# Moving weight loads and small steps between the units of a fused adaLN attention and gated MLP kernel

## The chip, the cores and the metric

The kernel runs on one core of a Trainium2 chip. The metric is the device time of one execution in microseconds. Before the change it was 1273.58 us, the median of three runs (1273.51 to 1275.47).

Engine names in profiles: PE multiplies matrices (PEld loads its weights), DVE is the vector engine, ACT the scalar engine, POOL is GpSimd. SP only issues DMAs here. Each engine works through its own list of instructions in order.

## The reference

The shapes are: 2048 rows of width D = 448; H = 16 heads of width 256 with 2048 cached keys and values each; a hidden width of 1792 in the MLP. Everything is bf16.

```
mod = (silu(c) @ w_mod) in six parts: sa, ca, ga, sb, cb, gb
h = layernorm(x) * (1 + ca) + sa
q = h @ wq, by heads;  p = softmax(q @ K^T / 16);  o = p @ V
x = x + ga * (o @ wo)
h = layernorm(x) * (1 + cb) + sb
x = x + gb * ((gelu(h @ w_gate) * (h @ w_up)) @ w_down)
```

## The kernel before

**Units.** The rows fall into four chunks of 512 (`r`). A unit `u` is one head `h` on one chunk: 64 units, the four chunks of a head next to each other. A unit has 16 steps `j`, one for each 128 keys. In a step the PE computes transposed scores `st` for two steps ahead (L321, two matmuls), ACT makes `E = exp(st)` (L462), the DVE adds E to `esum` (L503), and the PE multiplies V by E into two PSUM tiles `oT` (L506, two matmuls). At the end of a unit the DVE and ACT copy one oT tile each to `oTn` (L468, L469), and `esum` makes a trip through DRAM to be transposed: `scr<-esum` (L473), `esT<-scr` (L478).

**Behind the unit.** In the next unit the row sums are taken at step 7 (`inv`, L482), and the output projection follows in four tiles (`wo_tile`: matmuls L330, an add into x_acc on the DVE, L335) at steps 8, 10, 12 and 14. So the projection of a unit lies one unit behind its attention.

**Order.** The program's order on each engine is written out by hand. `fill(u, j, f)` puts a piece of work `f` behind the matmuls of step j of unit u; pieces of one slot run in the order in which they were filed. In the same way `mf(r, k, f)` puts a piece behind tile k of chunk r in the MLP. A step's pieces run before its `wo_tile`. At step 15 the query projection for the same chunk of the next head runs (`q_proj`, L307, eight matmuls); the last head has no next one, so its four units have none.

**PSUM tiles** come from pools: three of the tag `st`, two of `oT`, three of `mi`. The tiles of q_proj, wo_tile and of the modulation all use `mi`.

**Norms.** A norm of a chunk is split in pieces: `stats` (four, DVE), `rstd` (POOL), `norm` (four, DVE), `twin` (DVE), then either `transpose` on the PE or `turn`, and `modulate` (four, DVE, L268). `turn` is a trip through DRAM on SP's queue: `xscr<-xn` (L259) and four transposing loads `hT<-xscr` (L262), each of which waits for that store. Chunk 0 and 1 of the first norm use the PE; chunk 2 is turned at step 1 of unit 1 and wanted at step 12 and 13 of it, chunk 3 likewise in unit 2. The second norm's chunk 0 and 1 are done in units 62 and 63, chunk 2 and 3 in the MLP.

**Loads.** All but two early loads go through SP's queue. `load_wm` loads columns of w_mod; the first 960 are loaded at once, and the rest right behind the first head's K. `ld` (L410) loads K of head h+1 by two transposing DMAs at step 0 of the first unit of head h; `ld2` (L413) loads V and wo of head h+1 and wq of head h+2 one unit later. wq's load includes a small memset on POOL. `mod_rep` (L205) makes ga or gb from w_mod, `scale_wo` (L137) multiplies wo by ga on POOL, `mod_cols` (L184) makes sb and cb.

**MLP.** For each chunk, 14 tiles of 128 hidden columns are made in pairs by `gate_up`: gate and up matmuls (L543 with 64 rows, L550), gelu on ACT (L555), the product on the DVE (`hhT`, L556). The gate tile uses the tag `st`; the up tile uses `oT`, but every third, counted by `nu`, uses `mi`. Then `down` multiplies by w_down (L563) in four tiles. The first pair of the next chunk (`lead`) is put ahead of `down`. The last unit's output projection lies within the first chunk of the MLP.

Of the kernel before, what the change touches and what calls it, by code (L numbers as in the profile page):

```python
# [17 lines left out]
def kernel(  # L18
# [15 lines left out]
    nc = tc.nc  # L34
    S = A_x.shape[1]
    D = A_x.shape[2]
# [9 lines left out]
    NHC = Df // P  # L46
# [22 lines left out]
        fill=0.0, base=0, channel_multiplier=1,  # L69
# [6 lines left out]
    WA = 2 * D + 64  # L76
# [4 lines left out]
    x_acc = [res.tile([P, 4, D], F32, name=f"x_acc{r}") for r in range(NC)]  # L81
# [22 lines left out]
    def load_wq(h):  # L104
        wq_t = wts.tile([P, DCH, Dh], BF16, name="wq_t")
        nc.gpsimd.memset(wq_t[DL:P, 3, :], 0.0)
        nc.sync.dma_start(
            out=wq_t[:, 0:3, :],
            in_=A_wq[0:384, h * Dh:(h + 1) * Dh].rearrange("(c p) d -> p c d", p=P),
        )  # L110
        nc.sync.dma_start(out=wq_t[:DL, 3, :], in_=A_wq[384:D, h * Dh:(h + 1) * Dh])
        return wq_t
# [24 lines left out]
    def scale_wo(wo_t):  # L137
        for cc in range(2):
            nc.gpsimd.tensor_tensor(out=wo_t[:, cc, :], in0=wo_t[:, cc, :], in1=ga_bf[:], op=ALU.mult)  # L139

    def load_x(eng, r):
        eng.dma_start(
            out=x_bf[r], in_=x2d[r * 512:(r + 1) * 512, :].rearrange("(t p) d -> p t d", p=P)
        )

    def load_wm(a, b):
        nc.sync.dma_start(out=wm[:, 0:3, a:b], in_=w_mod[0:384, a:b].rearrange("(c p) n -> p c n", p=P))
        nc.sync.dma_start(out=wm[:DL, 3, a:b], in_=w_mod[384:D, a:b])
# [7 lines left out]
    wq[0] = load_wq(0)  # L156
    kTs[0] = load_k(0, parts=2)
    wos[0] = load_wo(0)
    load_wm(WA, 6 * D)
    load_x(nc.sync, 2)  # L160
    load_x(nc.sync, 3)
    wq[1] = load_wq(1)


    cps = mi_tile([P, DCH], F32, "cps")
# [18 lines left out]
    def mod_cols(g0):  # L184
        mps_ = mi_tile([P, 2 * DCH], F32, "modc")
        for v in range(2):
            for m in range(DCH):
                o = (g0 + v) * D + m * P
                for k in range(DCH):
                    nc.tensor.matmul(  # L190
                        mps_[:, v * DCH + m:v * DCH + m + 1],
                        lhsT=wm[:, k, o:o + P], rhs=scT[:, k:k + 1],
                        start=(k == 0), stop=(k == DCH - 1),
                    )
        return mps_

    def mod_cols_out(mps_, s_c, c1p_c):
        nc.vector.tensor_copy(out=s_c[:], in_=mps_[:, 0:DCH])
        nc.vector.tensor_single_scalar(out=c1p_c[:], in_=mps_[:, DCH:2 * DCH], scalar=1.0, op=ALU.add)
        nc.vector.tensor_copy(out=s_c[DL:P, 3:4], in_=mps_[0:DL, 3:4])  # L200
        nc.vector.tensor_single_scalar(
            out=c1p_c[DL:P, 3:4], in_=mps_[0:DL, 2 * DCH - 1:2 * DCH], scalar=1.0, op=ALU.add
        )

    def mod_rep(g, tgt):  # L205
        mp = mi_tile([P, D], F32, "mp")
        for k in range(DCH):
            nc.tensor.matmul(
                mp[:], lhsT=scT_rep[:, k, :], rhs=wm[:, k, g * D:(g + 1) * D],
                start=(k == 0), stop=(k == DCH - 1),  # L210
            )
        nc.vector.tensor_copy(out=tgt[:], in_=mp[:])
# [114 lines left out]
    def wo_tile(h, r, t, oTn, inv):  # L327
        wps = mi_tile([P, D], F32, "wps")
        for dc in range(2):
            nc.tensor.matmul(  # L330
                wps[:], lhsT=oTn[:, dc, t * P:(t + 1) * P], rhs=wos[h][:, dc, :],
                start=(dc == 0), stop=(dc == 1),
            )
        prev = x_bf[r] if h == 0 else x_acc[r]
        nc.vector.scalar_tensor_tensor(  # L335
            out=x_acc[r][:, t, :], in0=wps[:], scalar=inv[:, t:t + 1],
            in1=prev[:, t, :], op0=ALU.mult, op1=ALU.add,
        )
# [19 lines left out]
    fills = {}  # L358

    def fill(u, j, f):  # L360
        fills.setdefault((u, j), []).append(f)
# [4 lines left out]
            nc.vector.tensor_copy(out=scT_rep[:, k, :], in_=scT[:, k:k + 1].to_broadcast((P, P)))  # L366

    fill(0, 11, rep)
    fill(0, 13, lambda: mod_rep(2, ga_bf))
    fill(0, 14, lambda: scale_wo(wos[0]))  # L370
    fill(3, 10, lambda: mod_rep(5, gb_bf))
    fill(4, 9, lambda: mod_cols_out(mod_cols(3), sb_c, cb1p_c))

    def add_ln(key, src, c1p, s, js, jn, jt, jm=None):
        box = {}

        def stats(t):
            if t == 0:
                box["l"] = LN(key, src, c1p, s, mi_tile)
            box["l"].stats(t)  # L380

        for t in range(4):
            fill(*js[t], lambda t=t: stats(t))
        fill(*js[3], lambda: box["l"].rstd(0, 4))
        for t in range(4):
            fill(*jn[t], lambda t=t: box["l"].norm(t))
        fill(*jn[3], lambda: box["l"].twin(nc.vector))
        if jm is None:
            for p_ in range(2):
                fill(*jt[p_], lambda p_=p_: box["l"].transpose(p_))  # L390
        else:
            fill(*jt, lambda: box["l"].turn())
            for ch in range(DCH):
                fill(*jm[ch], lambda ch=ch: box["l"].modulate(ch))

    def at(u, *js):
        return [(u, j) for j in js]
# [9 lines left out]
    for u, (h, r) in enumerate(units):  # L407
        if h + 1 < H:
            if r == 0:
                def ld(h=h):  # L410
                    kTs[h + 1] = load_k(h + 1)

                def ld2(h=h):  # L413
                    vs[h + 1] = load_v(h + 1)
                    wos[h + 1] = load_wo(h + 1)
                    if h + 2 < H:
                        wq[h + 2] = load_wq(h + 2)
                fill(u, 0, ld)
                fill(u + 1, 0, ld2)
            if r == 3:  # L420
                fill(u, 0, lambda h=h: scale_wo(wos[h + 1]))
            fill(u, 15, lambda h=h, r=r: q_proj(h + 1, r))
        if h == H - 1 and r in (2, 3):
            jm = at(u + 1, 4, 6, 8, 10) if r == 2 else [("mlp", ch) for ch in range(DCH)]
            add_ln(("b", r - 2), x_acc[r - 2], cb1p_c, sb_c, at(u, 0, 2, 4, 6), at(u, 8, 9, 10, 11),
                   (u, 11), jm)


    mlpw = {}
# [61 lines left out]
    pend = None  # L491
    for u, (h, r) in enumerate(units):
        oT = [aps.tile([P, 512], F32, tag="oT", bufs=2, name=f"oT{i}") for i in range(2)]
        esum = espool.tile([P, 512], BF16, name="esum")
        for j in range(NKS):
            g = u * NKS + j
            emit_st(g + 2)
            emit_exp(g + 1)
            E = Es[g]
            if j == 1:  # L500
                nc.vector.tensor_tensor(out=esum[:], in0=Es[g - 1][:], in1=E[:], op=ALU.add)  # L501
            elif j > 1:
                nc.vector.tensor_tensor(out=esum[:], in0=esum[:], in1=E[:], op=ALU.add)  # L503
            Es.pop(g - 1, None)
            for i in range(2):
                nc.tensor.matmul(  # L506
                    oT[i][:], lhsT=vs[h][:, j, i * P:(i + 1) * P], rhs=E[:],
                    start=(j == 0), stop=(j == NKS - 1),
                )
            if j == NKS - 1:  # L510
                oTn, sums = finish_unit(u, oT, esum)
            for f in fills.pop((u, j), ()):
                f()
            if pend is not None:
                ph, pr, po, psums = pend[:4]
                if j == 7:
                    pinv = psums()
                if j in (8, 10, 12, 14):
                    wo_tile(ph, pr, (j - 8) // 2, po, pinv)
                if j == 14:  # L520
                    pend = None
        pend = (h, r, oTn, sums)


    wgu, wd = mlpw["gu"], mlpw["d"]

    nu = [0]

    def gate_up(r, fc0, hhT):
        hr = hT[("b", r)]  # L530
# [46 lines left out]
    def mf(r, k, f):  # L577
        mfill.setdefault((r, k), []).append(f)

    ph, pr, po, psums = pend  # L580
    box = {}
    mf(0, 5, lambda: box.update(inv=psums()))
    for t in range(4):
        mf(0, 5 + 1 + t, lambda t=t: wo_tile(ph, pr, t, po, box["inv"]))
        mf(0, NHC - 4 + t, fills.pop(("mlp", t))[0])
    for r in range(2, NC):
        for t in range(4):
            mf(r - 2, NHC + t, lambda r=r, t=t: ln2(r).stats(t))
            mf(r - 1, 3 + t, lambda r=r, t=t: ln2(r).norm(t))
            mf(r - 1, NHC - 2 + t // 2, lambda r=r, t=t: ln2(r).modulate(t))  # L590
        mf(r - 1, 2, lambda r=r: ln2(r).rstd(0, 4))
        mf(r - 1, 6, lambda r=r: (ln2(r).twin(nc.vector), ln2(r).turn()))
    lns = {}

    def ln2(r):
        if r not in lns:
            lns[r] = LN(("b", r), x_acc[r], cb1p_c, sb_c, mi_tile)
        return lns[r]
# [48 lines left out]
```

The softmax here doesn't subtract the row's maximum and nothing guards it: scores larger than these inputs give would overflow.

## Time and profile before

| what | value |
|---|---|
| median of three runs | 1273.58 us |
| the profiled execution's own time | 1273.87 us |
| its span, first to last instruction | 1272.1 us |
| mean granted PE clock | 0.996 |
| idle PE in the stretch 0 to 36 us | 9.3 us |
| 36 to 62 us (clock 0.90) | 7.3 us |
| 62 to 84.7 us (clock 0.97) | 0.5 us |
| 84.7 to 1078.5 us | 0.8 us |
| 1078.5 to 1124.7 us | 0.7 us |
| 1124.7 to 1133.2 us (clock 0.80) | 3.2 us |
| 1133.2 to 1228.2 us | 4.2 us |
| 1228.2 to 1272.1 us | 3.3 us |

The idle times are the length of each stretch less the busy time of the PE in it. The stretches are: unit 0 and what leads to it; unit 1; unit 2; units 3 to 60; 61 to 63; the first pair of the MLP; its first three chunks; the last chunk.

How to read what follows. In a list of waits a line names who waited, for what, and then the total in us, the number of times and the longest. In a timeline a line gives the start, the length, the engine (SPq is SP's queue), the line of the kernel, the operation, what it writes and reads, and how often; in brackets the idle time before it and what ended it. Matmuls overlap, so the time between two starts says more than the length of one: 0.216 us is the usual distance for 512 columns, and 0.427 us at half clock. Buffer numbers such as oT_511 tell apart the tiles of one name.

### The profile page before, as it was taken

To read this page: it belongs to the slowest core of one execution; us is meant where nothing else is said; L and a number is where in the kernel's file an instruction comes from. 1 tells how busy PE (TensorE), PEld (TensorE's weight loads), DVE (VectorE), ACT (ScalarE), POOL (GpSimd) and SP (SyncE) were. 2 spreads that over 40 slices of the span, in tenths; PEclk is the share of its full clock that TensorE was granted. 3 is DMA by queue.
4 is the path that set the end of the run, shared out by engine and by line. 5 is a ranking of instruction groups with operands and counts; after the bars stand their busy time and mean duration, and the time that the engine had idled before them with its cause. 6 is when DMAs were issued, how large, how long until landed. Compare 5 with 4: busy or idle time off the path is not lost.

```text
span 1272.1 us, 17345 instructions
## 1 busy us (share of the span) xinstructions
PE 1242.7 (98%) x5900; PEld 562.5 (44%) x5900; DVE 797.2 (63%) x1697; ACT 705.4 (55%) x1217; POOL 69.6 (5%) x87
## 2 busy tenths in 40 slices
PE   7799999999999999999999999999999999989998
PEld 3344444444444444444444444444444444434443
DVE  6666666656666666666666666666666666765543
ACT  4455656665655666666566666556666666642222
POOL 1100000000102001010000000000000000000000
PEclk9899999999999999999999999999999999999999
DMA  9312122372204040312222221304040310120110
GB/s 255 90 50 64 51 47 61 50 212 45 73 16 91 17 98 17 85 30 51 61 46 65 51 64 29 87 13 94 17 98 18 72 36 13 38 59 15 48 44 19
DMA packets 180170, 75.98 MB, mean 60 GB/s; under 512 B 149873, under 2 KB 170546, under 8 KB 180082
## 3 DMA queue, kind: packets, MB, share of 16 engines
q1 hardware_dynamic: 179024, 73.38, 24.5%
q10 hardware_dynamic: 1058, 1.51, 0.5%
q8 instruction: 46, 0.75, 0.2%
q14 instruction: 42, 0.34, 0.1%
HBM read 33.18 MB, written 13.37 MB: 37 GB/s over the span
## 4 chain that ended last, share of the span: by engine, by line
PE 92%; DVE 3%; DMA 3%; issue 1%; SPq 1%; ACT 1%; POOL 0%; DVEq 0%
PE st L321 33%; PE qps L307 8%; PE wps L330 7%; PE dps L563 3%; PE g_ps L550 3%; PE u_ps L550 3%; DMA scr<-esum 1%; PE g_ps L543 1%; DVE esum L503 1%; DMA wm<-in_w_mod_dram 0%; DMA xscr<-xn 0%; DMA esT<-scr 0%; DVE hT L268 0%; DVE bst L225 0%; SPq L262 0%
## 5 line engine op out<-in xcount | busy, mean ns | idle before, releaser
L462 ACT ACTIVATE E<-st 128x512 bf16<-128x512 f32 x1024 | 598.2, 599 | 287.4 <-PE st L321 277.4
L321 PE MATMUL st<-qT,kT 128*128 128x512 bf16 x2048 | 609.6, 379 | 1.1 <-ACT qT L314 1.1
L503 DVE TENSOR_TENSOR esum<-esum,E 128x512 bf16<-128x512 bf16 x896 | 394.5, 440 | 126.1 <-ACT E L462 93.3
L506 PEld LDWEIGHTS <-v_h 128*128 128x128 bf16 x2048 | 200.2, 98 | 247.5 <-issue 13.8
L321 PEld LDWEIGHTS <-kT 128*128 128x128 bf16 x2048 | 200.1, 98 | 232.0 <-issue 5.4
L330 PE MATMUL wps<-wo_t,oTn 128*128 128x448 bf16 x512 | 138.9, 353 | 0.0
L307 PE MATMUL qps<-hT,wq_t 128*128 128x512 bf16 x512 | 125.0, 385 | 5.7 <-DVE hT L268 5.2
L555 ACT ACTIVATE gl<-g_ps 128x512 bf16<-128x512 f32 x56 | 33.4, 597 | 98.1 <-PE g_ps L550 98.1
L314 ACT CAST qT<-qps 128x512 bf16<-128x512 f32 x64 | 37.5, 585 | 86.2 <-PE qps L307 86.2
L139 POOL TENSOR_TENSOR wo_t<-wo_t,ga_bf 128x448 bf16<-128x448 bf16 x32 | 34.9, 1110 | 889.3 <-DMA wo_t<-in_A_wo_dram 823.3
L307 PEld LDWEIGHTS <-wq_t 128*128 128x128 bf16 x512 | 50.5, 99 | 68.8 <-issue 10.5
L330 PEld LDWEIGHTS <-oTn 128*128 128x128 bf16 x512 | 50.2, 98 | 60.7 <-issue 0.6
L501 DVE TENSOR_TENSOR esum<-E 128x512 bf16<-128x512 bf16 x64 | 27.1, 423 | 75.5 <-ACT E L462 75.5
L556 DVE TENSOR_TENSOR hhT<-gl,u_ps 128x512 bf16<-128x512 bf16 x56 | 38.5, 687 | 48.2 <-PE u_ps L550 48.2
L335 DVE SCALAR_TENSOR_TENSOR x_acc_93<-wps,inv,x_acc_93 128x448 f32<-128x448 f32 x60 | 41.0, 684 | 40.7 <-PE wps L330 40.7
L335 DVE SCALAR_TENSOR_TENSOR x_acc_94<-wps,inv,x_acc_94 128x448 f32<-128x448 f32 x60 | 41.0, 684 | 40.3 <-PE wps L330 40.3
L335 DVE SCALAR_TENSOR_TENSOR x_acc_92<-wps,inv,x_acc_92 128x448 f32<-128x448 f32 x60 | 41.0, 684 | 38.6 <-PE wps L330 38.6
L335 DVE SCALAR_TENSOR_TENSOR x_acc_91<-wps,inv,x_acc_91 128x448 f32<-128x448 f32 x60 | 40.8, 681 | 29.7 <-PE wps L330 29.6
L550 PEld LDWEIGHTS <-wgu 128*128 128x128 bf16 x336 | 30.9, 99 | 49.0 <-issue 16.8
L312 DVE CAST qT<-qps 128x512 bf16<-128x512 f32 x64 | 44.2, 690 | 9.1 <-PE qps L307 3.2
L482 DVE TENSOR_REDUCE inv<-esT 128x4 f32<-128x512 bf16 x64 | 43.5, 680 | 7.8 <-DMA esT<-scr 7.8
L550 PE MATMUL g_ps<-hT,wgu 128*128 128x512 bf16 x168 | 46.3, 385 | 0.0
(329 smaller groups left out, 1151.5 us busy)
## 6 DMA issues: line engine op xcount, KB each, us to landing
scr<-esum SPq DMA_DIRECT2D x64, 128.0 KB, 2.0
wo_t<-in_A_wo_dram SPq DMA_DIRECT2D x16, 224.0 KB, 6.3
wq_t<-in_A_wq_dram SPq DMA_DIRECT2D x16, 192.0 KB, 4.9
xscr<-xn SPq DMA_DIRECT2D x6, 512.0 KB, 2.9
out_dram<-ob SPq DMA_DIRECT2D x16, 112.0 KB, 1.7
wd<-in_B_w_down_dram SPq DMA_DIRECT2D x1, 1568.0 KB, 17.2
x_all<-in_A_x_dram SPq DMA_DIRECT2D x3, 448.0 KB, 6.4
wgu<-in_B_w_gate_dram SPq DMA_DIRECT2D x1, 1344.0 KB, 9.5
```

Of the source, the lines that this page charges most:

```text
L307: nc.tensor.matmul(qps[:], lhsT=wq[h][:, ch, dc * P:(dc + 1) * P], rhs=hr[:, ch, :], start=(ch == 0), stop=(ch == DCH - 1),)
L312: nc.vector.tensor_copy(out=qT[:, dc, :], in_=qps[:])
L321: nc.tensor.matmul(st[:], lhsT=kTs[h][:, dc, j * P:(j + 1) * P], rhs=qTs[(h, r)][:, dc, :], start=(dc == 0), stop=(dc == 1),)
L330: nc.tensor.matmul(wps[:], lhsT=oTn[:, dc, t * P:(t + 1) * P], rhs=wos[h][:, dc, :], start=(dc == 0), stop=(dc == 1),)
L335: nc.vector.scalar_tensor_tensor(out=x_acc[r][:, t, :], in0=wps[:], scalar=inv[:, t:t + 1], in1=prev[:, t, :], op0=ALU.mult, op1=ALU.add,)
L462: nc.scalar.activation(out=E[:], in_=sts.pop(g)[:], func=ACTF.Exp, scale=inv_sqrt_dh)
L482: nc.vector.tensor_reduce(out=inv[:], in_=esT[:], axis=mybir.AxisListType.X, op=ALU.add)
L503: nc.vector.tensor_tensor(out=esum[:], in0=esum[:], in1=E[:], op=ALU.add)
L506: nc.tensor.matmul(oT[i][:], lhsT=vs[h][:, j, i * P:(i + 1) * P], rhs=E[:], start=(j == 0), stop=(j == NKS - 1),)
L550: nc.tensor.matmul(ps[fc, i][:], lhsT=wgu[:, 3 * i + ch, fc * P:(fc + 1) * P], rhs=hr[:, ch, :], start=False, stop=(ch == 2),)
L556: nc.vector.tensor_tensor(out=hhT[:, fc, :], in0=gl[:], in1=ps[fc, 1][:], op=ALU.mult)
L563: nc.tensor.matmul(dps[:], lhsT=hhT[:, fc, t * P:(t + 1) * P], rhs=wd[:, fc, :], start=(fc == 0), stop=(fc == NHC - 1),)
```

## The change

- **Loads.** At the start only columns 960 to 1344 of w_mod follow the first K; the other 1344 columns are loaded at step 0 of unit 3. wq of head 1 is loaded ahead of the last chunk of x. For head 0 alone, `ld` (K of head 1) moves from unit 0 to unit 1, and `ld2` (V and wo of head 1, wq of head 2) from unit 1 to unit 2.
- **Modulation.** ga and the scaling of the first wo move from steps 13 and 14 of unit 0 to steps 3 and 4 of unit 1; gb moves from unit 3 to unit 5, sb and cb from unit 4 to unit 6.
- **Output projection.** Its tiles run at steps 9, 11, 13 and 15. The last stands behind the query projection and is the last PE work of a unit.
- **Second norm.** In units 62 and 63 the statistics run at steps 1, 2, 4, 6, the norms at 7 to 10 and the turn at 10. In the MLP the norms of a chunk run behind tiles 2 to 5, the turn behind 5, and the modulates one by one behind 9, 10, 11 and 12; rstd is filed behind the last `down` tile.
- **First chunk of the MLP.** The row sums of unit 63 are taken behind tile 4, its four wo tiles behind 5 to 8. `nu` starts at 2.

```diff
-    load_wm(WA, 6 * D)
+    load_wm(WA, 3 * D)
     load_x(nc.sync, 2)
+    wq[1] = load_wq(1)
     load_x(nc.sync, 3)
-    wq[1] = load_wq(1)
...
-    fill(0, 13, lambda: mod_rep(2, ga_bf))
-    fill(0, 14, lambda: scale_wo(wos[0]))
-    fill(3, 10, lambda: mod_rep(5, gb_bf))
-    fill(4, 9, lambda: mod_cols_out(mod_cols(3), sb_c, cb1p_c))
+    fill(1, 3, lambda: mod_rep(2, ga_bf))
+    fill(1, 4, lambda: scale_wo(wos[0]))
+    fill(3, 0, lambda: load_wm(3 * D, 6 * D))
+    fill(5, 4, lambda: mod_rep(5, gb_bf))
+    fill(6, 4, lambda: mod_cols_out(mod_cols(3), sb_c, cb1p_c))
...
-                fill(u, 0, ld)
-                fill(u + 1, 0, ld2)
+                fill(u + (h == 0), 0, ld)
+                fill(u + 1 + (h == 0), 0, ld2)
...
-            add_ln(("b", r - 2), x_acc[r - 2], cb1p_c, sb_c, at(u, 0, 2, 4, 6), at(u, 8, 9, 10, 11),
-                   (u, 11), jm)
+            add_ln(("b", r - 2), x_acc[r - 2], cb1p_c, sb_c, at(u, 1, 2, 4, 6), at(u, 7, 8, 9, 10),
+                   (u, 10), jm)
...
-                if j in (8, 10, 12, 14):
-                    wo_tile(ph, pr, (j - 8) // 2, po, pinv)
-                if j == 14:
-                    pend = None
+                if j in (9, 11, 13, 15):
+                    wo_tile(ph, pr, (j - 9) // 2, po, pinv)
...
-    nu = [0]
+    nu = [2]
...
-    mf(0, 5, lambda: box.update(inv=psums()))
+    mf(0, 4, lambda: box.update(inv=psums()))
     for t in range(4):
-        mf(0, 5 + 1 + t, lambda t=t: wo_tile(ph, pr, t, po, box["inv"]))
-        mf(0, NHC - 4 + t, fills.pop(("mlp", t))[0])
+        mf(0, 5 + t, lambda t=t: wo_tile(ph, pr, t, po, box["inv"]))
+        mf(0, 9 + t, fills.pop(("mlp", t))[0])
     for r in range(2, NC):
         for t in range(4):
             mf(r - 2, NHC + t, lambda r=r, t=t: ln2(r).stats(t))
-            mf(r - 1, 3 + t, lambda r=r, t=t: ln2(r).norm(t))
-            mf(r - 1, NHC - 2 + t // 2, lambda r=r, t=t: ln2(r).modulate(t))
-        mf(r - 1, 2, lambda r=r: ln2(r).rstd(0, 4))
-        mf(r - 1, 6, lambda r=r: (ln2(r).twin(nc.vector), ln2(r).turn()))
+            mf(r - 1, 2 + t, lambda r=r, t=t: ln2(r).norm(t))
+            mf(r - 1, 9 + t, lambda r=r, t=t: ln2(r).modulate(t))
+        mf(r - 2, NHC + 3, lambda r=r: ln2(r).rstd(0, 4))
+        mf(r - 1, 5, lambda r=r: (ln2(r).twin(nc.vector), ln2(r).turn()))
```

## The prediction

> **What bounds the kernel now.** I read the page first, then the waits of the PE, then the timelines of the stretches in which the PE waits. The profiled execution took 1273.87 us, of which 1272.1 are the span and 1.77 lie around it; it stands 0.3 us above the median of the three timed runs (1273.58). The sum below is made against 1273.87.
>
> ```profile
> span 1272.1 us, 17345 instructions
> PE 1242.7 (98%) x5900; PEld 562.5 (44%) x5900; DVE 797.2 (63%) x1697; ACT 705.4 (55%) x1217; POOL 69.6 (5%) x87
> ```
>
> The PE bounds all of it. The change takes no matmul away, so it can only win time in which the PE stands still or runs slowly. The PE's waits (total, times, longest) say where:
>
> ```profile
> PE qps L307 <- DVE hT L268: 5.2, 3, 2.7
> PE g_ps L543 <- DVE hT L268: 4.2, 3, 1.5
> PE u_ps L543 <- DVE oTn L468: 2.9, 1, 2.9
> PE oT_511 L506 <- DVE oTn L468: 1.8, 1, 1.8
> PE oT_3048 L506 <- DVE oTn L468: 0.7, 1, 0.7
> ```
>
> The reader sees four places: the late third chunk in unit 1 (5.2), the first unit border (1.8), the step from attention to the MLP (2.9), and the three chunk borders in the MLP (4.2). The first is fed by SP's queue:
>
> ```profile
> 38.88 0.39 SPq L473 DMA_DIRECT2D scr<-esum  x1
> ...
> 42.46 0.82 SPq L127 DMA_DIRECT2D v_h<-in_A_v_cache_dram  x1
> ...
> 46.46 0.53 SPq L259 DMA_DIRECT2D xscr<-xn  x1
> 51.81 5.07 SPq L262 DMA_TRANSPOSE hT<-xscr  x4
> ...
> 105.74 3.94 SPq L119 DMA_TRANSPOSE kT<-in_A_k_cache_dram  x2
> ```
>
> V, wo and wq of the next head stand in front of the store of the normalized rows (xscr); the hT transposes wait for that. The last line prices a pair of K transposes on a quiet queue. One more loss is in no list of waits, because matmuls overlap: in the PE timeline the second PV pair of a unit starts late.
>
> ```profile
> 104.74 0.59 PE L321 MATMUL st<-qT,kT 128*128 128x512 bf16 x2
> 105.21 0.38 PE L506 MATMUL oT_1107<-E,v_h 128*128 128x512 bf16 x1
> 105.43 0.38 PE L506 MATMUL oT_1108<-E,v_h 128*128 128x512 bf16 x1
> 105.64 0.59 PE L321 MATMUL st<-qT,kT 128*128 128x512 bf16 x2
> 106.07 0.38 PE L506 MATMUL oT_1107<-E,v_h 128*128 128x512 bf16 x1
> ```
>
> From st to PV is 0.47 us here and 0.43 everywhere else. This 0.04 stands at the start of every unit that follows a query projection (43 of 43 units between 300 and 1040 us).
>
> **What the Trainium skill says.** "TensorE: Matmul & The Clock Gate", Part 1: an idle window of about 3.4 us halves the PE's clock, and about as much busy time restores it. The trace agrees: after the hole at 52 to 58 us, matmuls start 0.427 us apart instead of 0.216 until 63.5, and after the 2.9 us hole at 1125.4 again until 1131.5. "DMA: Bandwidth & Descriptors", Issuing engines are not separate DMA queues: all DMAs share the same 16 engines. The trace agrees: xscr lands 5.33 us after its issue behind V, and 2.94 on quiet queues (68.53). "Trainium Kernel Development and Optimization", Performance Expectations: matmul busy time tells little of the distance to the roof; here it hides that 0.04.
>
> **Part by part.** *Unit 0.* The gate's projection leaves (PE 0.76, its DVE cast 0.62), and so does the wo scaling on POOL, beside which a DVE norm took 1.10 instead of 0.39 and an esum 1.25 instead of 0.42. So the last norm's statistics end 1.2 earlier, the esum 2.7 earlier (36.15, not 38.88), and oT_511's 1.8 us wait falls away. The projection returns in unit 1, step 3; ahead of wo_tile at step 9 it has five steps of 0.86, against 0.76 + 0.6 + 2.05 (POOL). wq of head 1 now leads the last x load: both are long landed. POOL's other moved step, wq's memset of 0.31 ahead of the load, goes one unit later with it, behind nothing that waits.
>
> *Unit 1.* SP now has the K transposes in front of xscr, 3.94 in place of the 3.9 us of V, wo, wq: xscr goes 7.25 us after the esum store, where it was 7.58. The K transposes land 4.5 to 4.7 after issue, the last 9.9 after the esum store, so xscr lands at 10.2 (quiet, 2.94) to 12.6 (5.33 again); I take 11.2, against 12.9. The fourth hT lands 6.55 later in both. With the 2.7 from unit 0, hT is complete near 36.15 + 17.75 = 53.9 instead of 58.3. The PE arrives at about 50 (52.25 before, less 2.7 from unit 0, plus 0.76 for the projection, less one wo tile) and still waits some 4 us with three matmuls in it. The fourth starts at 54.5, and four more at 0.43 end at 56.7, where 60.9 stood: it leaves unit 1 about 4.5 ahead.
>
> *Unit 2.* V, wo and wq now precede xscr of the fourth chunk, which had a free queue (esum store 64.84, last hT 77.97: 13.1 later). With unit 1's old order this becomes 7.58 + 5.33 + 6.55 = 19.5. The PE wants it 14.6 to 15.6 after the store (before: 79.45). So the stall of unit 1 is repeated: the modulate and the fourth matmul at 20.0, four more at 0.43 and a wo tile to 22.3, where the projection ended 16.8 after the store (81.66) and the store itself now comes 0.7 sooner against the PE (no add before it): 22.3 - 16.8 - 0.7 = 4.8, less the 0.4 of a wait for qT that the wo tile covers, 4.5 in all. Units 0 to 2 together: 0, with +2.5 (slower) to -4.5 (no new stall) as ends. Behind the late modulates on the DVE stand only esums, with eight E buffers.
>
> *w_mod's rest* at unit 3: two issues of 0.5 on SP behind esT with nothing after them until the next unit, 1.2 MB (near 4 us at the 290 GB/s of V's load). Its users at units 5 and 6 come 30 us later, theirs at unit 20 and 62. The same matmuls, elsewhere: 0. Without that cover it would be a 4 us stall.
>
> *The last wo tile at the border*, 2 x 0.189 = 0.38 of PE work after the projection. The 0.04 comes from E of the next unit, queued on ACT behind the qT copy, which waits for the projection; 0.38 covers it: 57 x 0.042 = 2.4 won. Bounds: 0 if E slides too, 2.5 at most. Three borders without a projection show 0.62 where 0.38 is normal (ACT oTn): 3 x 0.24 = 0.7 won. Also the DVE casts oTn ahead of one 0.68 add, which takes most of the 0.7 stall at 293: 0.6 won. The DVE idles 1.29 there, so the add costs nothing; without that room it would be 0.68 a unit.
>
> *Into the MLP.* From 1124.70 to 1133.17 the first pair of gate and up takes 8.47; later pairs take 3.24. With nu = 2 its u tiles are an mi buffer and the oT buffer that ACT frees. The DVE's oTn (now near 1127.4) is asked for only by the third tile, at about 1127.6. So 5.2 less at most; I take 4.8, as the first u tile waits up to 0.5 for an add on the DVE. Against it: inv is asked for one tile earlier in a stream 5 us earlier, while its sums stand in SP's queue behind xscr and four hT (12.7 us from xscr at 1123.7, so 1136.4). The DVE blocks behind hhT of tile 4 from 1133.3; the PE runs on with what PSUM it has and stops at the third wps, about 1.1. Net 3.7.
>
> *Chunk borders in the MLP.* Starts show excesses of 1.3, 1.6 and 1.6 (1557, 1879, 1880 ns where 0.3 is normal). Modulates now follow tiles 9 to 12 instead of 10 to 13 or 12, 12, 13, 13. The norms and the turn come one tile earlier: xscr near 1177.2 instead of 1179.14, hT at 1182.5 to 1186.5, wanted at 1182.9 to 1188.0. All in time, the first by 0.4. The last modulate ends while tile 13's matmuls run. 3.9 of 4.2 won.
>
> Sum: 0 + 2.4 + 0.7 + 0.6 + 3.7 + 3.9 = 11.3; 1273.9 - 11.3 = **1262.6**.
>
> **The rivals.** *Both head stalls in full* (13%): the K transposes take the 8.9 us they took at 21 us instead of 3.94, and xscr 5.33: 6.3 more, 1268.9. For it: those transposes did. Against: the DMA engines are idle from 33 to 38 us. *The MLP gives little* (14%): the blocked inv costs 3 instead of 1.1, and the first modulates wait for hT and hold hhT: 1.1 + 2 less, near 1266. For it: the margin of 0.4. *No stall in unit 2* (10%): xscr overtakes V's packets and the PE waits little: 1262.6 - 4.5 = 1258. Against: unit 1 now. *Slower* (5%): at 60 borders the last wps is the third mi buffer in a row. If the DVE's add of the tile two steps before is late, the PE waits; the slack is 3.8 - 1.3 = 2.5 us, and the change turns into a loss once the wait is over 11.3/60 = 0.19 us a border. At 0.25: 1262.6 + 15 = 1277.6. Against: the DVE idles 0.56 to 1.3 us several times a unit. That the change does not do what it says is not open: the built order on SP has K, xscr in unit 1 and V, wo, wq, xscr in unit 2.
>
> **The numbers.** Forecast 58%, 1260 to 1265.5 by the bounds of its terms. To leave out no more than two in ten, the range goes from 1258.5 (most of the case without a stall) to 1269.5 (most of the full head stalls). A measurement tells 0.2%, 2.5 us, from no change, so faster means below 1271.0: 58 + 14 + 10 and most of 13 make 92%; within 4%, slower 4%.
>
> **What would show it.** Right: oT_511's wait gone; a wait of qps on hT in unit 2 as well as unit 1; 0.43 from st to PV at each unit start; the first pair of the MLP in under 4 us at full clock; a DVE wait for esT of about 3 us near 1133; g_ps waits for hT near 0. Wrong: no wait in unit 2, a wait of PE wps for the DVE at the borders, or u_ps still waiting for oTn.

## The result and the profile after

The changed kernel takes 1262.14 us (median of four runs, 1260.60 to 1263.66), 0.9908 of the time before (95% interval 0.9891 to 0.9925); 1262.6 was forecast. A second set of its runs gave 1261.01 us and 0.9892 (0.9879 to 0.9906). It is faster by about 1%. One execution of the kernel with extra matmuls, further down, took 2207.82 us at a granted clock of 0.558, where all others on record have 0.995 to 1.000; it enters no ratio. The profiled execution took 1262.72 us, 1261.0 of them the span.

The page of the changed kernel, its head:

```profile
span 1261.0 us, 17310 instructions
PE 1239.4 (98%) x5900; PEld 562.7 (45%) x5900; DVE 804.7 (64%) x1697; ACT 711.8 (56%) x1217; POOL 69.4 (6%) x87
```

The number of matmuls is the same, and the PE's busy share still reads 98%: that share would not have told that 11 us went. The PE's waits of the changed kernel (total, times, longest) do:

```profile
PE qps L307 <- DVE hT L268: 8.1, 7, 1.9
...
PE oT_3049 L507 <- ACT E L463: 0.3, 1, 0.3
PE u_ps L542 <- DVE x_acc_93 L335: 0.3, 1, 0.3
PE wps L330 <- DVE x_acc_94 L335: 0.3, 1, 0.3
```

The waits of g_ps for hT, of u_ps and of oT_511 for oTn are gone from the list. The wait of qps for hT has grown from three pieces to seven: it is now there in unit 1 and in unit 2. SP's queue in the changed kernel shows why:

```profile
34.91 0.39 SPq L474 DMA_DIRECT2D scr<-esum  x1
...
38.09 5.64 SPq L119 DMA_TRANSPOSE kT<-in_A_k_cache_dram  x2
43.83 0.53 SPq L259 DMA_DIRECT2D xscr<-xn  x1
47.48 5.03 SPq L262 DMA_TRANSPOSE hT<-xscr  x4
59.27 0.38 SPq L474 DMA_DIRECT2D scr<-esum  x1
...
62.83 0.83 SPq L127 DMA_DIRECT2D v_h<-in_A_v_cache_dram  x1
...
66.96 0.53 SPq L259 DMA_DIRECT2D xscr<-xn  x1
72.08 5.08 SPq L262 DMA_TRANSPOSE hT<-xscr  x4
```

In unit 1 the K transposes stand in front of the row store, in unit 2 V, wo and wq. Before, unit 2 had nothing in front of it.

Because matmuls overlap, I compare stages by the starts of matching matmuls: the first PV matmul of a unit, the first matmul of an MLP pair. The differences add up to that of the two spans, 11.1 us.

| stage, us | before | after | won | forecast |
|---|---|---|---|---|
| up to the first PV matmul | 17.51 | 16.27 | 1.2 | 0 |
| units 0, 1, 2 | 19.83, 29.28, 19.84 | 19.07, 26.30, 25.91 | -2.3 | 0 |
| units 3 to 59 | 976.88 | 974.07 | 2.8 | 2.4 + 0.6 |
| units 60 to 62 | 47.23 | 46.47 | 0.8 | 0.7 |
| unit 63 and the first MLP pair | 22.59 | 18.03 | 4.6 | 4.8 |
| pairs 2 to 6 of the first chunk | 17.68 | 18.09 | -0.4 | -1.1 |
| the three chunk borders with what lies between | 74.07 | 69.69 | 4.4 | 3.9 |
| the last chunk | 47.23 | 47.10 | 0.1 | 0 |

The start of a unit in the changed kernel's PE timeline, at the same place as the one shown of before:

```profile
104.18 0.59 PE L321 MATMUL st<-qT,kT 128*128 128x512 bf16 x2
104.61 0.38 PE L507 MATMUL oT_1103<-E,v_h 128*128 128x512 bf16 x1
104.83 0.38 PE L507 MATMUL oT_1104<-E,v_h 128*128 128x512 bf16 x1
105.04 0.59 PE L321 MATMUL st<-qT,kT 128*128 128x512 bf16 x2
105.47 0.38 PE L507 MATMUL oT_1103<-E,v_h 128*128 128x512 bf16 x1
```

From 105.04 to 105.47 is 0.43 us, no longer 0.47. For the first MLP pair the stretches read (bounds, length, busy time and count of PE, PEld, DVE, ACT, POOL, then the granted PE clock), before the change:

```profile
1124.70:1133.20 8.50, 5.26 (x19) 1.62 (x20) 4.51 (x10) 3.04 (x4) 0.00 (x0) 0.80 0.39 108
```

and after it:

```profile
1122.20:1126.10 3.90, 3.61 (x17) 1.28 (x16) 3.69 (x9) 2.74 (x4) 0.00 (x0) 1.00 0.39 134
```

Some 8.5 us at clock 0.80 became 3.9 at full clock. The price of asking for the sums sooner is there too, in the changed kernel's DVE timeline

```profile
1134.77 0.69 DVE L483 TENSOR_REDUCE inv<-esT 128x4 f32<-128x512 bf16 x1 [2.61 <-DMA esT<-scr]
```

and, much smaller, on its PE:

```profile
1136.91 0.54 PE L330 MATMUL wps<-wo_t,oTn 128*128 128x448 bf16 x2 [0.25 <-DVE x_acc_94 L335]
```

So the total was met within half a microsecond. That it came so near is luck: the four runs lie over 3 us, and two rows of the table that were forecast at 0, the start (+1.2) and the first three units (-2.3), cancel in part. The experiments take both up, and test the rest by undoing one part at a time.

### The profile page after: what moved, and what is told of

The parts are those of the page before. It is cut to its first block, busy times and chain, and to the rows that moved or that the text cites. A ratio compares the mean times of both kernels' runs of the same rounds, so it can differ in the third digit from the quotient of the medians.

```text
span 1261.0 us, 17310 instructions
## 1 busy us (share of the span) xinstructions
PE 1239.4 (98%) x5900; PEld 562.7 (45%) x5900; DVE 804.7 (64%) x1697; ACT 711.8 (56%) x1217; POOL 69.4 (6%) x87
## 4 chain that ended last, share of the span: by engine, by line
PE 91%; DVE 3%; DMA 3%; issue 1%; SPq 1%; ACT 1%; POOL 0%; DVEq 0%
PE st L321 32%; PE qps L307 9%; PE wps L330 7%; PE dps L562 3%; PE g_ps L549 3%; PE u_ps L549 3%; DVE esum L504 1%; DMA scr<-esum 1%; PE g_ps L542 1%; DMA xscr<-xn 1%; DMA esT<-scr 1%; DVE bst L225 1%; SPq L262 1%; DMA hT<-xscr 0%; ACT E L463 0%
## 5 line engine op out<-in xcount | busy, mean ns | idle before, releaser
L463 ACT ACTIVATE E<-st 128x512 bf16<-128x512 f32 x1024 | 604.4, 598 | 299.4 <-PE st L321 291.2
L549 PE MATMUL u_ps<-hT,wgu 128*128 128x512 bf16 x168 | 45.4, 379 | 0.0
```

The costliest lines, as they stand in the source:

```text
L463: nc.scalar.activation(out=E[:], in_=sts.pop(g)[:], func=ACTF.Exp, scale=inv_sqrt_dh)
L549: nc.tensor.matmul(ps[fc, i][:], lhsT=wgu[:, 3 * i + ch, fc * P:(fc + 1) * P], rhs=hr[:, ch, :], start=False, stop=(ch == 2),)
```

## The experiments

Theory 1 for the head of the kernel: what stands in front of the row store in SP's queue makes the holes. Rivals: late norm pieces on DVE and POOL (theory 2), or the shared DMA engines whatever the order (theory 3). For the rest, the sum of the prediction is the theory. Every kernel below is the changed kernel with the one edit shown; ratios are against the kernel before.

### The loads of head 1 back in units 0 and 1

```diff
-                fill(u + (h == 0), 0, ld)
-                fill(u + 1 + (h == 0), 0, ld2)
+                fill(u, 0, ld)
+                fill(u + 1, 0, ld2)
```

> Only K, V, wo of head 1 and wq of head 2 go back to units 0 and 1. Theory 1 (what stands ahead of the row store in SP's queue makes the holes): unit 2 has no hole and takes about 20 us instead of 25.9; unit 1 keeps its hole, with V ahead, at 26 to 28; about 5 us faster than the changed kernel, near 1257. Theory 2 (the holes come from late norm pieces on DVE and POOL, wherever the loads stand): unit 2 keeps a hole of 4 to 6 us, time near 1262.

Measured: 1257.43 us, 0.9858 (0.9841 to 0.9874). Units 1 and 2 take 28.21 and 19.54 us. The hole of unit 2 is gone, that of unit 1 stays. Theory 2 falls: the norm pieces are as in the changed kernel. And this part of the change is shown to be a loss: without it the kernel is 3.6 to 4.7 us faster than the changed kernel in its two sets of runs.

### The loads of head 1 behind the turns

```diff
-                fill(u + (h == 0), 0, ld)
-                fill(u + 1 + (h == 0), 0, ld2)
+                fill(u + (h == 0), 2 * (h == 0), ld)
+                fill(u + 1 + (h == 0), 2 * (h == 0), ld2)
```

> K of head 1 at step 2 of unit 1, V, wo and wq at step 2 of unit 2, both behind the turn in SP's queue. Theory 1: both holes go, units 1 and 2 take about 20 us each, 11 us faster than the changed kernel, near 1251. Theory 2: holes stay, near 1262. Theory 3 (the DMA engines are shared, so order in the queue does not help): the hT loads land late, at least half of both holes stays, 1256 or more.

Measured: 1252.63 us, 0.9825 (0.9807 to 0.9842), the fastest form but for the last one below, which equals it. Its SP queue:

```profile
35.55 0.39 SPq L474 DMA_DIRECT2D scr<-esum  x1
...
38.77 0.54 SPq L259 DMA_DIRECT2D xscr<-xn  x1
41.87 5.03 SPq L262 DMA_TRANSPOSE hT<-xscr  x4
46.94 5.47 SPq L119 DMA_TRANSPOSE kT<-in_A_k_cache_dram  x2
...
59.65 0.37 SPq L259 DMA_DIRECT2D xscr<-xn  x1
62.58 5.04 SPq L262 DMA_TRANSPOSE hT<-xscr  x4
68.07 0.82 SPq L127 DMA_DIRECT2D v_h<-in_A_v_cache_dram  x1
```

and what is left of the wait:

```profile
PE qps L307 <- DVE hT L268: 1.6, 3, 1.0
```

The store goes out 3.2 us after the sums' store in unit 1 instead of 8.9. Units 1 and 2 take 21.68 and 19.54 us. Of the 1.6 us that are left, 1.3 lie in unit 1, and there the DVE's own order holds up the PE, not the loads: the last hT had landed at 49.1, and from then on the DVE waited for nothing until all four modulates were done. Statistics and a sum stand between the second modulate and the third:

```profile
49.21 0.73 DVE L268 TENSOR_SCALAR hT<-hT,ca1p_c,sa_c 128x512 bf16<-128x512 bf16 x2
49.85 0.62 DVE L225 BATCH_NORM_STATS2 bst<-x_all 128x6 f32<-128x448 bf16 x1
...
50.91 0.73 DVE L268 TENSOR_SCALAR hT<-hT,ca1p_c,sa_c 128x512 bf16<-128x512 bf16 x2
```

So theory 1 explains the two large holes, and a small rest is of the kind that theory 2 named.

### V alone behind the turn

```diff
-                fill(u + 1 + (h == 0), 0, ld2)
+                fill(u + 1 + (h == 0), 2 * (h == 0), ld2)
```

> Only V, wo and wq go behind the turn in unit 2; K stays ahead of it in unit 1. Theory 1: the hole of unit 2 goes, that of unit 1 stays: 6 us faster than the changed kernel, near 1256. Theory 2 and 3: near 1262.

Measured: 1257.92 us, 0.9861 (0.9845 to 0.9878). Unit 1 takes 26.37, unit 2 19.54. The two holes are separate, and each goes with its own load.

### V on ACT's queue

V is issued by ACT at step 0 of unit 2; wo and wq, in a piece `ld3` of their own, by SP behind the turn.

```diff
-                    vs[h + 1] = load_v(h + 1)
+                    vs[h + 1] = load_v(h + 1, nc.scalar if h == 0 else nc.sync)
...
+                fill(u + 1 + (h == 0), 2 * (h == 0), ld3)
```

> K ahead of the turn in unit 1 as in the changed kernel; in unit 2 V is issued from ACT's queue at step 0, wo and wq on SP behind the turn. Theory 1 (the place in SP's queue alone): the row store goes out 3.8 us earlier, the hole of unit 2 goes, unit 2 takes 19.6, as with all three behind the turn. Theory 3 (the shared DMA engines): V's 1 MB still runs in front of the row store and delays its landing by 2 us or more; hT is 2 us late, and a hole of 1 to 2 us stays in unit 2 (21 us).

Measured: 1258.60 us, 0.9869 (0.9856 to 0.9883); unit 2 takes 20.31 us, between the two expectations. Its SP queue in unit 2:

```profile
57.51 0.37 SPq L477 DMA_DIRECT2D scr<-esum  x1
...
62.78 0.37 SPq L259 DMA_DIRECT2D xscr<-xn  x1
68.17 5.03 SPq L262 DMA_TRANSPOSE hT<-xscr  x4
```

The store lands 5.3 us after its issue, as behind V on one queue, against 2.9 on quiet engines. So both hold: the issue was 2.4 us sooner (5.3 after the sums' store, not 7.7), and sharing the engines took 2.4 on landing. Of the hole, 0.8 us are left.

### The changed kernel once more

> The changed kernel once more, for the spread of its units 1 and 2. If the length at half clock is luck: unit 2 takes anything from 21.8 to 26 us, and units 1 and 2 together 48 to 52.3; if the first profile showed a fixed cost: 25.9 again, within 0.2.

Measured: 1261.01 us, 0.9892 (0.9879 to 0.9906). Units 1 and 2 take 26.97 and 21.80 us in its profile, where the first profile had 26.30 and 25.91. In both the sums' store of unit 1 is at 59.3 and the fourth projection matmul of unit 2 at 79.0 to 79.1: the hole of unit 2 ends at the same time. It begins 1.5 us later in the second, as the PE arrives later. The clock behind it differs too, in the first profile

```profile
73.00:87.00 14.00, 10.38 (x34) 3.81 (x33) 6.17 (x13) 2.88 (x6) 0.31 (x1) 0.76 0.21 47
```

and in the second:

```profile
74.00:86.00 12.00, 9.62 (x44) 4.07 (x42) 7.54 (x15) 4.41 (x8) 0.31 (x1) 1.00 0.24 54
```

From that matmul to the first PV matmul of unit 3 it is 8.5 us in one and 6.0 in the other, the same work. So half clock after this hole costs 0 or up to 2.5 us. Whether it comes is not luck alone. Take the time from the end of the last PE work ahead of a hole to the fourth projection matmul, behind which the PE runs without a hole again; only three single matmuls lie in it. These are its lengths, with the number of matmuls that then follow at the distance of half clock (0.43 us for 512 columns, 0.37 for 448):

| kernel | unit 1: stretch, at half clock | unit 2: stretch, at half clock |
|---|---|---|
| before | 6.75 us, 7 | 1.06 us, 0 |
| changed, first profile | 5.97 us, 6 | 5.02 us, 12 |
| changed, second profile | 5.15 us, 13 | 3.43 us, 0 |
| wo tiles back | 4.99 us, 7 | 5.01 us, 4 |
| modulates back | 4.84 us, 10 | 4.07 us, 8 |
| nu from 0 | 4.89 us, 12 | 3.45 us, 0 |
| gate back in unit 0 | 5.99 us, 13 | 3.49 us, 0 |

In the six profiles with both holes the two are tied together: the more matmuls run at half clock in unit 1, the later the PE reaches the hole of unit 2, and the shorter that stretch is. Behind stretches below 3.5 us no half clock follows. What stays luck here is the number at half clock behind a long stretch, which does not follow its length.

Five profiles with these loads (the two, and the kernels with nu, modulates or wo tiles undone) give units 0 to 2 in 71.3, 67.8, 67.4, 69.0 and 70.3 us, 69.1 in the mean; before, with one profile, it is 68.95.

### Extra matmuls in the holes

39 matmuls on constant data, never read, keep the PE busy in both holes.

```diff
+        busy = {2: (8, 6, 5, 2), 3: (4, 5, 4, 5)}.get(r, (0,) * 4) if h == 0 else (0,) * 4
...
+            if dc == 0 and sum(busy):
+                dm = mi_tile([P, 512], F32, "dm")
...
+                for _ in range(busy[ch] if dc == 0 else 0):
+                    nc.tensor.matmul(dm[:], lhsT=id_bf[:], rhs=wm[:, 0, 0:512], start=True, stop=True)
```

> The changed kernel with 39 extra 512-column matmuls put into the two holes (8, 6, 5, 2 ahead of the four first projection matmuls of unit 1; 4, 5, 4, 5 in unit 2), whose result nobody reads; the holes stay as long. Theory (half clock after the hole is part of the price, and its length is luck): no matmul at half clock after the holes, unit 2 takes about 21.8 us, unit 1 no longer than 26.3; about 3 us faster than the changed kernel, near 1259, and less spread. Rival (the hole alone is the price): the same as the changed kernel or slower by up to 2 us.

Measured: 1264.56 us, 0.9920 (0.9904 to 0.9935): slower, a miss. The stretches over the two holes:

```profile
47.00:61.00 14.00, 13.92 (x66) 6.32 (x65) 10.10 (x24) 4.31 (x8) 1.55 (x3) 1.00 0.23 48
72.00:86.00 14.00, 11.85 (x55) 5.09 (x53) 6.66 (x15) 3.26 (x6) 0.31 (x1) 1.00 0.23 48
```

The clock is full in both, and unit 1 takes 24.35 us, 2.0 and 2.6 less than in the two profiles of the changed kernel. But in unit 2 (25.46) one hT landed 4.4 us after its issue where 2.7 is usual, and the five extra matmuls behind the third projection matmul held the fourth by 0.9 us. And later, at the MLP, this kernel lost 1.7 + 0.8 us that the changed one does not lose, waiting for mi tiles (u_ps and wps for the DVE's adds: 1.2 and 1.6 us); the two extra mi tiles may have shifted which tile waits for which, but that was not tried. So it shows that busy matmuls keep the clock, and not what that is worth.

### The output projection tiles back

```diff
-                if j in (9, 11, 13, 15):
-                    wo_tile(ph, pr, (j - 9) // 2, po, pinv)
+                if j in (8, 10, 12, 14):
+                    wo_tile(ph, pr, (j - 8) // 2, po, pinv)
```

> Only the four output projection tiles go back to steps 8, 10, 12 and 14. Theory of the sum (the tile at the border covers ACT's late E): the 0.04 us returns at every unit start with a query projection (2.2 us), the three 0.24 us holes of the last head (0.7) and part of the wait at 293 us (0.6) return: 3 to 3.5 us slower than the changed kernel, near 1265.5. Rival (the border tile is worth nothing, the 0.04 is a fixed cost of a new unit): within 1 us of 1262.

Measured: 1266.54 us, 0.9929 (0.9914 to 0.9945). Units 3 to 59 take 977.33 us instead of 974.07, units 60 to 62 take 47.23 instead of 46.47. The 0.47 is back (here two PV matmuls share a line):

```profile
104.92 0.59 PE L321 MATMUL st<-qT,kT 128*128 128x512 bf16 x2
105.39 0.59 PE L507 MATMUL oT<-E,v_h 128*128 128x512 bf16 x2
105.82 0.59 PE L321 MATMUL st<-qT,kT 128*128 128x512 bf16 x2
106.25 0.60 PE L507 MATMUL oT<-E,v_h 128*128 128x512 bf16 x2
```

The theory holds, the rival falls: the border tile is worth 3.3 + 0.8 us.

### The counter nu from 0

```diff
-    nu = [2]
+    nu = [0]
```

> Only nu starts at 0 again, so the first two up tiles both take oT buffers. Theory of the sum: the second one waits for the DVE's oTn (free at 1125.8 in the changed kernel, wanted at 1122.9), a hole of about 2.6 us, then half clock for the rest of the first pair (12 matmuls, 2.5 us), less the 0.6 us of stall at the third wps that the later stream then hides: 4 to 4.5 us slower than the changed kernel, near 1266.5. Rival (the regrouped norms alone brought oTn forward enough): at most 1 us slower.

Measured: 1264.09 us, 0.9915 (0.9901 to 0.9929). The wait it was meant to bring back:

```profile
PE u_ps L542 <- DVE oTn L469: 2.7, 1, 2.7
```

The rival falls: the regrouped norms do not bring oTn forward enough. But the stage grew by 2.6 us, not 4 or more, and 0.4 of it came back at the third wps. The half clock that I had added did not appear in the profile: the pair ran at clock 1.00 behind a hole of 2.7 us. The profiled run, 1262.40 us, is the fastest of the four; the others took 1263.93 to 1264.38 us, and without a profile of them it stays open where they lost the 1.5 to 2 us more.

### The modulates back

```diff
-            mf(r - 1, 9 + t, lambda r=r, t=t: ln2(r).modulate(t))
+            mf(r - 1, NHC - 2 + t // 2, lambda r=r, t=t: ln2(r).modulate(t))
...
-        mf(0, 9 + t, fills.pop(("mlp", t))[0])
+        mf(0, NHC - 4 + t, fills.pop(("mlp", t))[0])
```

> Only the modulates of the MLP go back to tiles 10 to 13 (second chunk) and 12, 12, 13, 13 (third and fourth); norms and turn stay one tile earlier. Theory of the sum: the three holes at the chunk borders return, 1.2 + 1.6 + 1.6 = 4.4 us slower than the changed kernel, near 1266.5. Rival (the earlier turn did it): no slower than 1263.

Measured: 1265.41 us, 0.9928 (0.9915 to 0.9940). The wait is back to what it was:

```profile
PE g_ps L542 <- DVE hT L268: 4.2, 3, 1.5
```

The stage takes 74.07 us again instead of 69.69, 4.4 us. The place of the modulates did it, not the earlier turn, which this kernel keeps.

### The gate back in unit 0

```diff
-    fill(1, 3, lambda: mod_rep(2, ga_bf))
-    fill(1, 4, lambda: scale_wo(wos[0]))
+    fill(0, 13, lambda: mod_rep(2, ga_bf))
+    fill(0, 14, lambda: scale_wo(wos[0]))
```

> Only the gate projection and the first wo scaling go back to steps 13 and 14 of unit 0. Theory of the sum: the wait of oT in the first border returns (1.8) and the esum store, with all that follows it on SP, comes 2.7 us later, so that hT of the third chunk does too: 2.7 us slower than the changed kernel, near 1265. Rival (the hole of unit 1 swallows it, because the K loads set its end): within 0.5 us of the changed kernel.

Measured: 1263.15 us, 0.9908 (0.9893 to 0.9923), within the spread of the changed kernel. The wait of oT for the DVE at the first border is back, 1.8 us; it is the longer of the two that this line counts:

```profile
PE oT L507 <- DVE oTn L469: 2.3, 2, 1.8
```

The sums' store of unit 0 comes 21.36 us after the first PV matmul instead of 18.64, 2.7 later as expected. Units 0 and 1 take 48.85 us together, where the five profiles above have 45.1 to 46.0, so 3.4 more than their mean at the start of unit 2. Unit 2 takes 21.86. Against the two of the five whose unit 2 also ran at full clock (67.4 and 67.8 for units 0 to 2) it is 70.7, about 3 more, near the 2.7 expected. The medians of the runs do not show it clearly, as the spread from the clock in units 1 and 2 is as large. So the mechanism is in the trace; its worth in the medians is open.

### Both loads behind the turns, and the sums later

```diff
-    mf(0, 4, lambda: box.update(inv=psums()))
+    mf(0, 6, lambda: box.update(inv=psums()))
...
-        mf(0, 5 + t, lambda t=t: wo_tile(ph, pr, t, po, box["inv"]))
+        mf(0, 7 + t, lambda t=t: wo_tile(ph, pr, t, po, box["inv"]))
```

> The loads of head 1 behind the turns, as in the run with both of them there, and in the first chunk of the MLP the row sums behind tile 6 and the wo tiles behind 7 to 10. Theory of the sum: the DVE no longer blocks 2.6 us for the sums, the PE's 0.4 us stall at the third wps goes: 0.4 us faster than that run, near 1252. Rival: another 0.4 us appears where the wo adds meet the modulates on the DVE; same as that run.

Measured: 1252.47 us, 0.9826 (0.9813 to 0.9839), the same as without the second edit. Pairs 2 to 6 of the first chunk lose 0.4 us of stall as expected (17.68 instead of 18.04), but the step into the MLP took 18.10 instead of 17.78. The time is that of the rival, but its reason is not shown: pairs 2 to 6, in which adds and modulates meet, lost their stall, and the stage behind them takes 69.69 us in both kernels. The step into the MLP takes 17.78 to 18.09 us in seven other profiles with the same code there, so a gain of 0.4 us is neither shown nor excluded.

## Why the prediction was right, and where two terms were off

- **Unit 0**: right. It lost the 0.76 us of the gate's projection, and the sums' store came 18.64 us after the first PV matmul, to the digit of the forecast.
- **Unit 1**: the mechanism was right; the term of the K transposes was mis-sized. "3.94 in place of the 3.9 us of V, wo, wq" became 5.64 us, so the store went out 8.9 us after the sums' store, not 7.25, and landed after 12.5, not 11.2. One row was too little to price it. The profile of before has 14 such pairs from 105 us on, of 3.94 to 5.71 us, and the row taken is the shortest. In the second profile of the changed kernel the pair took less:

```profile
38.97 4.62 SPq L119 DMA_TRANSPOSE kT<-in_A_k_cache_dram  x2
```

There the store went out after 7.9 us and landed after 11.8. The start of unit 2 came 3.7 and 3.1 us sooner after the first PV matmul in the two profiles, where "about 4.5" was forecast; the forecast's own times, 60.9 and 56.7, give only 4.2.
- **Unit 2**: the repeated stall is shown by three experiments, and its end was right (19.3 us after the sums' store against 19.5). The half clock behind it was put at a fixed length, four more matmuls; it was 12 matmuls in one profile of the changed kernel and none in the other, as the forecast did not ask how long the PE would then have stood. Over the five profiles with these loads units 0 to 2 scatter over 4 us, around a mean that is 0.2 above the one profile of before. The 0 of the forecast is near that mean, and within 2.5 us in the first profile.
- **Start**: 1.2 us that the forecast did not have. Some 1.05 of it is not of the change: seven of the first eight projection matmuls took 3.14 us in the profile of before and 2.09 in that of after; in the second profile of the changed kernel it is 3.15 again.
- **Border tile, last head**: right, with 2.8 + 0.8 against 3.0 + 0.7.
- **Into the MLP**: right in place, with 4.6 - 0.4 against 4.8 - 1.1. The kernel with nu from 0 shows that 2.6 of it are the wait itself. Before is 2.0 us longer than that kernel still: 1.5 us behind the wait, where its matmuls ran at half clock, and 0.5 us because the wait ended later. The stall behind the sums was forecast at 1.1 and is 0.4: the DVE waits 2.6 us for them where 3.1 were reckoned, and the PE, 0.3 us later out of the first pair, comes to the third wps that much later.
- **Chunk borders**: right, 4.4 against 3.9; I had left 0.5 for a rest that is not there.
- **The slower rival** (wps waiting for its mi buffer at each border) has no place in the changed kernel's list of waits but for one 0.25 us in the MLP. It came up at a like place in the kernel with extra mi tiles.

## What to carry to other kernels

When loads are moved to a quieter time, look at what waits behind them on the issuing queue: here loads issued one step ahead of a store held it up by 4 to 6 us, and putting the two groups of loads two steps later, behind the store and its transposes, was worth 8.4 to 9.5 us where the whole change was worth 11. Two matmuls of other work at a border can hide a 0.04 us lag that no list of waits names: 1.7 us over the 44 units from 16 to 59, lost again with the tile moved back, and so by estimate 2.2 us over all 57. Put a DVE step that the PE needs next ahead of the last product, not behind it, and ask which buffer's release a new stage needs first.

## What the runs showed of the hardware that was not expected

Half clock behind a hole can be foretold in part. In the twelve profiles of kernels without extra matmuls, and after their first 20 us, matmuls at half clock stand only behind the sparse stretches at the two holes and at the step into the MLP. All 14 stretches of 4.07 us or more were followed by 4 to 13 of them. The stretches of 3.55 us or less were followed by none. The two at the step into the MLP fit: 4.10 us before, 3.55 with nu from 0, though the longest waits in them, 2.9 and 2.7 us, are nearly the same. The Trainium skill, "TensorE: Matmul & The Clock Gate", Part 1, gives an idle window of about 3.4 us and calls it free-running, that is, not tied to the start of the kernel. The traces agree in size, and add that three single matmuls did not keep a stretch from counting as idle. That the free-running window is what spreads the 4 to 13 would fit, but no run here shows it.

A long half clock in unit 1 can also cost nothing: in the second profile of the changed kernel it only made the PE arrive later at unit 2's hole, which ended at the same time.
